# Sliding-window attention and a channel mix on one core: which transposes go through the DMA crossbar

## The chip, the cores and the metric

The kernel runs on one core of one Trainium2 chip. A core has five engines with instruction queues of their own: TensorE (PE, matrix products; its weight loads are listed apart as PEld), VectorE (DVE), ScalarE (ACT), GpSimd (POOL) and SyncE (SP), which here only issues DMAs. Sixteen DMA engines do the transfers. The metric is device microseconds of one execution; lower is better.

## The reference

Attention over four batches and eight heads with 768 positions of 64 values; a position sees itself and the 127 before it, and the first four positions of its batch ("sinks"). Its output, with the heads side by side as 512 columns, is the input x of a channel mix:

```python
scores = scale * np.matmul(q, k.transpose(0, 1, 3, 2))
keep = is_sink | in_window                       # rel >= 0 and rel < 128, or pos < 4
a = softmax(np.where(keep, scores, -1e9))
x = (a @ v)                                      # heads side by side: B x 768 x 512
xk = mu_k * x + (1.0 - mu_k) * x_prev            # x_prev: x of the position before
xr = mu_r * x + (1.0 - mu_r) * x_prev
k = np.maximum(xk @ w_k, 0.0)                    # 512 x 1024
v = k * k @ w_v                                  # 1024 x 512
r = 1.0 / (1.0 + np.exp(-(xr @ w_r)))            # 512 x 512
return r * v
```

## The kernel before

The work is cut into twelve units of 256 positions: unit u is part u % 3 of batch u // 3. For each unit the kernel does the following.

- **Loads.** k, q and v of the unit come in fp32 on SP's queue, two DMAs each (L404 v, L414 and L434 k and q), into `ks`, `qs`, `vs`, which have three buffers each.
- **Casts.** k, q and v are cast to bf16 (`kb`, `qb`, L619 and L626; `vb`, L681), in halves, each on ScalarE, VectorE or GpSimd.
- **Transposes of k and q.** The products need `kt` and `qt` with the 64 values of a head along the partitions. There are two ways. On TensorE: four 128x128 transposes for a half (L654) into a PSUM bank, and a copy out of it (L667) by ScalarE or VectorE; k and q then come in rows of 1 KB (L434). By the DMA crossbar: SP issues one transposing DMA for a half (L641); k and q then come in rows of 256 bytes (L414). `KD` and `QD` say for which units the second way is taken: k of units 4 to 11, q of units 8 to 11.
- **Attention.** Scores (`sc`, L749) two head pairs at a time, exponentials (`e`, L803, ScalarE), a mask (L817, VectorE), products with v (`o` in a bank, L836), a reciprocal (`rec`, L850) and the scaling into `x` (L853), both VectorE. There are four head pairs in a unit.
- **Transposes of x.** `mix` turns x into `xt`, the 512 columns along the partitions: on TensorE, four transposes for a half of x (L877) and a copy out of PSUM (L886, ScalarE or VectorE). The tuple `XD` could name units for the crossbar; it is empty here.
- **Mix.** VectorE forms `td`, the difference of neighbouring positions (L905, two per unit), and from it `xk` and `xr` (L916, four each).
- **Channel mix.** Key products (`kp`, L967), relu (`rl`, L977 ScalarE or L981 VectorE), square (`kk`, L989), gate products (`rp`, L998) with a tanh (`th`, L1004), value products (`vp`, L1016; the last quarter L937), a last combination (`ob`, L1025, L947), and stores on SP's queue (L1032, L952).

The five weight loads stand among the first loads; their casts to bf16 are spread over three engines (L584, L588, L590). Fillers, products of a tile of zeros (L1036), run on TensorE where it would stand in the first part of the kernel.

Every step is first recorded as an operation with a number, in program order. `ORDER` gives, for each engine, the numbers in the order in which that engine is to issue them; `CHOICE` gives the engine of an operation that has a choice; `Plan.schedule` replays the five lines against costs written in the file, only to settle which buffer each tile takes and where fillers go. Engines wait for each other through semaphores alone. So each queue runs strictly in its written order: an instruction that waits holds up all that stands behind it on its engine, and on SP a transposing DMA that waits for its source holds up the loads behind it.

Of the kernel before, what the change touches and what calls it, by code (L numbers as in the profile page):

```python
# [18 lines left out]
    92: "ACT", 93: "ACT", 94: "ACT", 98: "ACT", 102: "DVE", 103: "POOL", 106: "POOL",  # L19
    111: "DVE", 112: "DVE", 113: "ACT", 139: "DVE", 142: "POOL", 151: "ACT", 152:  # L20
    "DVE", 154: "DVE", 198: "DVE", 199: "POOL", 202: "POOL", 206: "ACT", 227: "DVE",
    286: "DVE", 287: "DVE", 288: "ACT", 320: "DVE", 356: "POOL", 358: "POOL", 360:
    "DVE", 366: "ACT", 367: "DVE", 436: "POOL", 438: "DVE", 443: "POOL", 446: "ACT",
    447: "ACT", 449: "DVE", 518: "DVE", 526: "ACT", 527: "ACT", 532: "DVE", 595:
    "POOL", 605: "ACT", 606: "ACT", 608: "DVE", 677: "POOL", 683: "DVE", 684: "ACT",
    686: "DVE", 755: "DVE", 759: "DVE", 761: "ACT", 762: "DVE", 774: "DVE", 830:
    "POOL", 836: "POOL", 838: "ACT", 839: "DVE", 856: "DVE", 916: "DVE", 919: "DVE",
    1014: "DVE", 1038: "DVE", 1042: "DVE",
}

KD = range(4, 12)
QD = range(8, 12)

XD = ()
# [4 lines left out]

BEGIN = {"SP": 800.0, "PE": 1260.0, "ACT": 800.0, "DVE": 930.0, "POOL": 930.0}  # L40

FUDGE = ((42000.0, 900.0), (1e12, 300.0))
# [7 lines left out]
SWITCH = 100.0  # L50

# [5 lines left out]
ORDER = {  # L57
    "PE": (
        104, 101, 88, 117, 107, 110, 115, 128, 120, 125, 143, 153, 131, 140, 136, 149,
        146, 169, 160, 167, 181, 221, 225, 222, 226, 233, 197, 234, 203, 170, 173,  # L60
        178, 182, 185, 190, 207, 249, 194, 214, 229, 230, 200, 251, 314, 306, 315,
        318, 307, 319, 239, 263, 252, 310, 260, 255, 237, 311, 241, 292, 322, 242,
        245, 264, 276, 267, 272, 246, 279, 326, 282, 327, 359, 299, 285, 334, 324,
        330, 364, 331, 345, 410, 382, 337, 390, 383, 386, 391, 342, 387, 412, 353,
        394, 368, 348, 395, 398, 375, 402, 439, 424, 403, 400, 462, 290, 463, 470,
        444, 471, 413, 492, 416, 425, 421, 433, 428, 406, 448, 407, 455, 504, 490,
        466, 474, 519, 467, 475, 480, 478, 529, 545, 549, 546, 550, 486, 524, 557,
        487, 558, 493, 573, 496, 505, 501, 513, 508, 553, 584, 554, 531, 561, 538,
        482, 576, 563, 483, 581, 569, 598, 570, 603, 651, 592, 565, 587, 607, 566,
        649, 663, 621, 633, 625, 614, 622, 626, 634, 639, 637, 629, 652, 630, 660,  # L70
        655, 699, 703, 700, 704, 664, 729, 727, 672, 667, 707, 711, 685, 712, 708,
        692, 641, 730, 741, 733, 738, 642, 645, 715, 766, 646, 780, 792, 781, 788,
        784, 789, 719, 793, 720, 785, 742, 808, 745, 750, 723, 717, 773, 724, 811,
        764, 819, 796, 816, 800, 798, 801, 854, 840, 858, 862, 855, 859, 863, 827,
        884, 882, 804, 866, 822, 805, 872, 867, 870, 847, 885, 896, 888, 893, 878,
        874, 879, 932, 940, 933, 875, 962, 897, 941, 900, 905, 936, 918, 937, 944,
        960, 925, 950, 945, 956, 948, 974, 963, 957, 1000, 966, 1001, 1008, 971, 1009,
        975, 978, 1004, 986, 983, 1005, 1012, 952, 993, 953, 1016, 1018, 1013, 1020,
        1028, 1024, 1032, 1021, 1029, 1025, 1033, 1036, 1040, 1037, 1041, 1048, 1046,
        1044, 1049, 1056, 1052, 1057, 1053,  # L80
    ),
    "DVE": (
        80, 81, 102, 89, 111, 112, 119, 124, 116, 121, 126, 122, 130, 127, 135, 139,
        154, 132, 133, 137, 155, 138, 158, 156, 159, 90, 91, 162, 157, 164, 163, 172,
        165, 166, 177, 189, 227, 198, 152, 184, 174, 179, 175, 180, 186, 191, 187,
        192, 236, 209, 210, 216, 211, 217, 218, 95, 212, 224, 228, 220, 219, 259, 320,
        254, 96, 97, 256, 257, 261, 213, 262, 232, 99, 271, 309, 266, 243, 321, 313,
        317, 268, 273, 269, 274, 247, 294, 287, 295, 297, 328, 360, 301, 286, 303,
        302, 336, 341, 296, 332, 298, 347, 338, 304, 339, 352, 343, 305, 344, 393,
        354, 385, 355, 349, 389, 350, 370, 397, 438, 373, 371, 377, 372, 378, 379,  # L90
        415, 404, 432, 291, 367, 420, 427, 417, 418, 422, 434, 423, 429, 435, 430,
        449, 518, 381, 380, 450, 408, 374, 451, 457, 453, 459, 458, 452, 465, 469,
        530, 473, 477, 500, 460, 512, 507, 495, 454, 488, 552, 497, 498, 502, 514,
        503, 515, 509, 461, 575, 510, 532, 580, 560, 548, 556, 533, 577, 591, 578,
        540, 536, 586, 534, 582, 484, 583, 542, 571, 535, 544, 541, 593, 588, 594,
        608, 543, 567, 589, 659, 654, 609, 537, 610, 616, 612, 618, 619, 611, 666,
        617, 636, 624, 656, 661, 657, 628, 662, 671, 632, 755, 683, 673, 674, 668,
        620, 669, 686, 737, 613, 732, 687, 706, 688, 694, 734, 739, 735, 695, 740,
        643, 696, 689, 690, 702, 647, 759, 698, 710, 768, 744, 714, 691, 771, 697,
        749, 769, 721, 746, 751, 747, 752, 815, 787, 810, 762, 783, 774, 725, 812,  # L100
        765, 775, 813, 770, 791, 795, 777, 817, 776, 818, 802, 772, 779, 821, 826,
        856, 828, 842, 861, 843, 829, 778, 865, 839, 823, 824, 806, 892, 857, 887,
        844, 869, 845, 889, 894, 890, 849, 850, 851, 852, 895, 846, 904, 853, 880,
        899, 876, 916, 935, 901, 906, 902, 907, 919, 970, 943, 920, 939, 927, 923,
        921, 928, 924, 947, 922, 929, 965, 958, 977, 967, 968, 972, 973, 982, 979,
        1011, 980, 1003, 984, 930, 985, 931, 988, 1007, 989, 995, 991, 996, 997, 954,
        990, 992, 1014, 999, 1015, 998, 1022, 1031, 1026, 1035, 1042, 1038, 1039,
        1043, 1050, 1058, 1054,
    ),
    "ACT": (  # L110
        77, 79, 78, 100, 105, 109, 123, 118, 108, 113, 129, 134, 148, 144, 145, 141,
        150, 147, 161, 176, 171, 168, 196, 188, 93, 223, 151, 183, 235, 204, 92, 193,
        208, 250, 215, 195, 231, 94, 258, 201, 253, 308, 316, 206, 240, 270, 265, 312,
        98, 293, 238, 323, 275, 278, 277, 281, 284, 363, 280, 283, 300, 361, 335, 340,
        325, 365, 288, 346, 411, 351, 441, 384, 392, 388, 414, 369, 396, 419, 376,
        399, 440, 431, 426, 401, 366, 464, 445, 472, 499, 516, 494, 446, 521, 456,
        526, 491, 511, 520, 468, 476, 481, 523, 506, 547, 551, 447, 525, 479, 675,
        559, 574, 579, 600, 605, 527, 555, 590, 539, 562, 585, 597, 564, 602, 599,
        604, 653, 658, 679, 650, 665, 606, 615, 681, 623, 635, 627, 640, 638, 753,
        631, 670, 701, 705, 728, 736, 731, 713, 693, 684, 709, 748, 743, 757, 716,  # L120
        761, 834, 767, 782, 790, 794, 814, 786, 809, 718, 832, 825, 797, 799, 838,
        820, 910, 908, 841, 860, 864, 886, 883, 912, 891, 873, 868, 914, 848, 903,
        871, 898, 934, 942, 969, 938, 961, 926, 964, 946, 951, 949, 976, 981, 1002,
        1010, 987, 1006, 994, 1017, 1019, 1030, 1034, 1045, 1047,
    ),
    "POOL": (
        87, 85, 86, 82, 103, 106, 83, 84, 114, 142, 202, 199, 205, 358, 356, 289, 436,
        443, 595, 677, 528, 830, 763, 836, 917,
    ),
    "SP": (  # L130
        1, 0, 2, 3, 4, 5, 8, 9, 6, 7, 10, 19, 20, 11, 12, 13, 17, 18, 14, 21, 22, 15,
        16, 23, 24, 25, 26, 31, 32, 27, 29, 30, 244, 28, 35, 37, 36, 357, 362, 33,
        437, 38, 442, 43, 333, 41, 34, 42, 39, 44, 248, 45, 40, 47, 517, 49, 53, 46,
        329, 522, 48, 51, 405, 596, 50, 676, 489, 601, 55, 54, 52, 56, 485, 61, 57,
        409, 678, 59, 680, 682, 60, 58, 67, 568, 63, 65, 66, 69, 62, 754, 756, 758,
        572, 760, 68, 64, 644, 71, 648, 73, 831, 835, 726, 833, 837, 70, 72, 722, 74,
        909, 803, 75, 807, 911, 913, 915, 76, 881, 877, 955, 1023, 959, 1027, 1051,
        1059, 1055,
    ),
}  # L140


class Plan:

    SEM = 60.0
# [8 lines left out]
    def op(self, engine, cost, emit, rank, reads=(), writes=(), take=(), hold=(), port=False,  # L161
           lag=None, service=0.0, descs=128, mode=0, alts=None, room=2080):
        i = len(self.ops)
# [8 lines left out]
    def schedule(self):  # L172
        ops = self.ops
# [918 lines left out]
```

## Time and profile before

| | |
|---|---|
| runs, us | 170.49, 172.09, 172.26; median 172.09 |
| profiled execution: span, us | 170.4 |
| TensorE busy | 160.5 us (94%), granted clock 0.988 in the mean |
| VectorE busy | 152.1 us (89%) |
| ScalarE busy | 127.3 us (75%) |
| GpSimd busy | 18.9 us (11%) |
| DMA | 33.82 MB, 199 GB/s in the mean |
| transposing DMAs | 16 for k, 8 for q, all on SP's queue |

The profile comes from one execution. A group's busy time counts overlapping instructions once; "mean" is the duration of one. TensorE's instructions are pipelined and their ends are modelled, so a run of matmuls is better priced by the chain of waits, which gives the time from one to the next. A stretch of the table by windows shows busy microseconds of each engine, the granted clock (PEclk) and the mean busy share of the 16 DMA engines, which can pass 1 where packets overlap. "Landing" is the time from the issue of a DMA to its last byte.

### The profile page before, as it was taken

What the parts mean: (1) busy time and instruction counts of PE and PEld (TensorE: products, weight loads), DVE (VectorE), ACT (ScalarE), POOL (GpSimd) and SP (SyncE); (2) the same over time, 40 slices, a digit from 0 to 9 for tenths busy, and PEclk for the clock granted to TensorE, in tenths of its full rate; (3) what the DMA queues carried; (4) which work ended last, traced back from release to release, by engine and by line L of the source; (5) the groups of instructions that cost most, each with busy time, mean ns of one, the idle gap of its engine ahead of it and who ended that gap; (6) DMA issues with size and microseconds to landing.
All of it is one profiled execution on the core that took longest, in us unless ns stands there. A gap on an engine that the chain in (4) does not pass through costs nothing.

```text
span 170.4 us, 4224 instructions
## 1 busy us (share of the span) xinstructions
PE 160.5 (94%) x1598; PEld 103.6 (61%) x1616; DVE 152.1 (89%) x393; ACT 127.3 (75%) x208; POOL 18.9 (11%) x44
## 2 busy tenths in 40 slices
PE   7986998899999999999999999979999999999992
PEld 2444476665658566767557785745575675765751
DVE  5197988999999899999999999898999999999562
ACT  3595799999899999999978989627597648842220
POOL 6720210101430200100020000201000020000000
PEclk9998799999999999999999999999999999999999
DMA  4999989899997999699899896949989750001313
GB/s 137 245 316 348 298 246 257 307 370 304 219 232 167 201 199 276 143 246 189 234 251 208 166 265 140 184 131 296 215 194 231 178 168 8 0 4 62 146 38 123
DMA packets 76803, 33.82 MB, mean 199 GB/s; under 512 B 63848, under 2 KB 71280, under 8 KB 76784
## 3 DMA queue, kind: packets, MB, share of 16 engines
q1 hardware_dynamic: 76768, 33.56, 80.9%
q8 instruction: 12, 0.20, 0.5%
q14 instruction: 7, 0.06, 0.1%
q10 hardware_dynamic: 16, 0.00, 0.0%
HBM read 24.12 MB, written 6.29 MB: 179 GB/s over the span
## 4 chain that ended last, share of the span: by engine, by line
PE 63%; DMA 11%; SPq 9%; DVE 8%; ACT 5%; issue 2%; DVEq 0%
PE bank L1016 18%; PE bank L967 17%; PE bank L998 10%; DMA qs<-in_q_dram 6%; PE sc L749 5%; PE bank L836 5%; DMA ks<-in_k_dram 3%; SPq L414 3%; SPq L404 2%; PE bank L877 2%; DMA qt<-qb 2%; ACT e L803 2%; PE bank L1036 2%; PE bank L654 2%; SPq L434 2%
## 5 line engine op out<-in xcount | busy, mean ns | idle before, releaser
L967 PE MATMUL bank<-xk,wk_sb 128*128 128x256 bf16 x384 | 51.0, 273 | 0.5 <-DVE xk L916 0.4
L803 ACT ACTIVATE e<-sc 128x1024 bf16<-128x1024 f32 (+1 forms) x48 | 44.6, 956 | 4.8 <-PE sc L749 4.7
L1016 PE MATMUL bank<-wv_h,kk 128*128 128x512 bf16 x172 | 45.5, 379 | 0.5
L967 PEld LDWEIGHTS <-wk_sb 128*128 128x128 bf16 x384 | 35.7, 98 | 10.3 <-issue 1.3
L977 ACT ACTIVATE rl<-bank 128x512 bf16<-128x512 f32 x42 | 24.4, 599 | 12.5 <-PE bank L967 10.4
L817 DVE TENSOR_TENSOR e<-e,mask 128x1024 bf16<-128x1024 bf16 (+1 forms) x48 | 30.4, 645 | 0.0
L1016 PEld LDWEIGHTS <-kk 128*128 128x128 bf16 x184 | 16.7, 98 | 13.7
L998 PE MATMUL bank<-wr_sb,xr 128*128 128x512 bf16 x90 | 23.7, 379 | 0.3
L916 DVE SCALAR_TENSOR_TENSOR xk<-td,mu_all,xt 128x256 bf16<-128x256 bf16 x48 | 23.8, 519 | 0.1
L916 DVE SCALAR_TENSOR_TENSOR xr<-td,mu_all,xt 128x256 bf16<-128x256 bf16 x48 | 22.6, 480 | 0.0
L1004 ACT ACTIVATE th<-bank 128x512 f32<-128x512 f32 x24 | 14.2, 604 | 9.0 <-PE bank L998 8.7
L989 DVE TENSOR_TENSOR kk<-rl 128x512 bf16<-128x512 bf16 x48 | 19.1, 415 | 0.7 <-ACT rl L977 0.6
L853 DVE TENSOR_TENSOR x<-bank,rec 128x256 bf16<-128x256 f32 x48 | 19.3, 414 | 0.3
L1025 DVE SCALAR_TENSOR_TENSOR ob<-th,bank 128x512 f32<-128x512 f32 x23 | 15.6, 679 | 3.1 <-ACT th L1004 1.4
L836 PE MATMUL bank<-vb,e 128*128 128x65 bf16 x352 | 16.4, 194 | 0.1
L836 PEld LDWEIGHTS <-e 128*128 128x128 bf16 x352 | 13.8, 97 | 3.3 <-issue 0.5
L749 PE MATMUL sc<-qt,kt 64*128 64x128 bf16 (+1 forms) x256 | 14.2, 242 | 1.2 <-DMA qt<-qb 1.1
L998 PEld LDWEIGHTS <-xr 128*128 128x128 bf16 x96 | 9.0, 98 | 8.9 <-issue 0.3
L749 PEld LDWEIGHTS <-kt 64*128 64x128 bf16 x256 | 9.3, 96 | 6.6 <-issue 4.0
L886 ACT COPY xt<-bank 128x512 bf16<-128x512 bf16 x17 | 10.0, 588 | 3.9 <-PE bank L877 3.8
L1036 PE MATMUL bank<-warm 128*128 128x512 bf16 x35 | 11.8, 485 | 1.1 <-DVE warm L1055 1.1
L905 DVE TENSOR_TENSOR td<-xt 128x512 bf16<-128x512 bf16 x24 | 10.0, 416 | 0.0
(78 smaller groups left out, 153.5 us busy)
## 6 DMA issues: line engine op xcount, KB each, us to landing
qs<-in_q_dram SPq DMA_DIRECT2D x24, 256.0 KB, 4.7
ks<-in_k_dram SPq DMA_DIRECT2D x24, 256.0 KB, 4.3
vs<-in_v_dram SPq DMA_DIRECT2D x24, 256.0 KB, 4.7
out_dram<-ob SPq DMA_DIRECT2D x23, 256.0 KB, 3.7
w<-in_moe_w_k_dram SPq DMA_DIRECT2D x2, 1024.0 KB, 10.5
w<-in_moe_w_v_dram SPq DMA_DIRECT2D x2, 1024.0 KB, 10.2
w<-in_moe_w_r_dram SPq DMA_DIRECT2D x1, 1024.0 KB
kt<-kb SPq DMA_TRANSPOSE x16, 4.0
```

The lines of the kernel that those rows point to most:

```text
L749: nc.tensor.matmul(out=sc[:, a, o0:o1], lhsT=lhs[rows], rhs=rhs[rows], start=u not in BIAS, stop=True, skip_group_check=u in BIAS)
L803: nc.scalar.activation(out=buf[ek][:, :, lo:], in_=buf[sck][:, :, lo:], func=AF.Exp, scale=scale)
L817: nc.vector.tensor_tensor(out=at, in0=at, in1=m, op=ALU.mult)
L836: nc.tensor.matmul(out=o[:, g, a, :], lhsT=e[:, a, e0:e0 + 128], rhs=rhs, start=(T == 0 and i == 0), stop=(i == len(blocks) - 1), skip_gro ...
L853: P.op("DVE", dve(256), lambda ok=ok, rk=rk, c=c: nc.vector.tensor_tensor(out=buf["x", u][:, :, 128 * c:128 * c + 128].rearrange("p g (a d ...
L916: nc.vector.scalar_tensor_tensor(out=buf[key][:, c, :], in0=buf[tk][:, i, :], scalar=mu[w][:, c:c + 1], in1=xt[:, c, t0 - 1:t0 + 255], op0 ...
L967: nc.tensor.matmul(out=ps[:, i, :], lhsT=wk_sb[:, c, 128 * f:128 * f + 128], rhs=xk[:, c, :], start=(c == 0), stop=(c == NC - 1), skip_gro ...
L977: nc.scalar.activation(out=buf[rk], in_=buf[psk].rearrange("p (i t) -> p i t", i=2), func=AF.Relu)
L989: P.op("DVE", dve(512, 0.52), lambda f2=f2, rk=rk: nc.vector.tensor_tensor(out=buf["kk", u][:, 2 * f2:2 * f2 + 2, :], in0=buf[rk], in1=buf ...
L998: nc.tensor.matmul(out=buf[psk], lhsT=buf["xr", u][:, c, 128 * g:128 * g + 128], rhs=wr_sb[:, c, :], start=(c == 0), stop=(c == NC - 1))
L1016: nc.tensor.matmul(out=buf[psk], rhs=wv_h[:, f, :], lhsT=buf["kk", u][:, f, 128 * g:128 * g + 128], start=(f == 0), stop=(f == NF - 1))
L1025: P.op("DVE", dve(512), lambda psk=psk, tk=tk, bk=bk: nc.vector.scalar_tensor_tensor(out=buf[bk], in0=buf[tk], scalar=1.0, in1=buf[psk], o ...
```

## The change

The three sets that choose the crossbar are changed, the tables of choices and orders are replaced, and the replay in `Plan.schedule` goes: one `ORDER` now lists all operations (negative numbers are fillers and their bank), and `SLOTS` gives the buffer of each tile. Cut to its core:

```diff
-KD = range(4, 12)
-QD = range(8, 12)
-
-XD = ()
+KD = range(5, 12)
+QD = (10, 11)
+
+XD = (5, 6, 7, 8, 9, 10, 11)
...
-    def schedule(self):
...
     def run(self):
-        for i in self.schedule():
-            if isinstance(i, tuple):
-                self.fill(i[1])
+        keys = [(name, key) for o in self.ops for name, key in o["take"]]
+        for (name, key), slot in zip(keys, SLOTS, strict=True):
+            self.buf[key] = self.pools[name][slot]
+        for i in ORDER:
+            if i < 0:
+                self.fill(self.pools["bank"][-1 - i])
             else:
                 self.ops[i]["emit"]()
```

For a unit in `XD`, the branch of `mix` that was not taken before is now taken. It issues two transposing DMAs, one for each 128 positions, each reading a whole row of x, so that both wait for all four head pairs:

```python
elif half == 0:
    for g in range(2):
        P.op("SP", 1240.0, lambda g=g: nc.sync.dma_start_transpose(
            out=xt[:, :, t0 + 128 * g:t0 + 128 * g + 128], in_=buf["x", u][:, g, :]),
            ...
            reads=[("x", u, c) for c in range(NP)],
```

Instructions by engine, before and after:

| engine | what | before | after |
|---|---|---|---|
| TensorE | transposes of x (L877) | 96 | 40 |
| | transposes of k and q (L654) | 96 | 120 |
| | fillers (L1036) | 35 | 30 |
| ScalarE | copies of x out of PSUM (L886) | 17 | 8 |
| | casts of k and q for the crossbar (L619) | 16 | 8 |
| | copies of k and q out of PSUM (L662, L667) | 19 | 22 |
| | casts of v (L681) | 14 | 12 |
| | relu (L977) | 42 | 45 |
| VectorE | copies of x out of PSUM (L886) | 7 | 2 |
| | casts of k and q (L619, L623, L626) | 5 | 11 |
| | copies of k and q out of PSUM (L662, L667) | 5 | 8 |
| | relu (L981) | 6 | 3 |
| GpSimd | casts of k, q, v and a weight | 15 | 21 |
| SP | loads in 256-byte rows, k and q (L414) | 24 | 18 |
| | loads in 1 KB rows, k and q from unit 1 (L434) | 20 | 26 |
| | transposing DMAs of k and q (L641) | 24 | 18 |
| | transposing DMAs of x (L897) | 0 | 14 |

One weight cast (`wk`) goes from ScalarE to GpSimd, one (`wv`) from VectorE to ScalarE. Line numbers are those of the kernel before. In the new order of SP's queue the first 16 loads stand as before. Around the x transposes (a pair each, here "x5" for unit 5) the queue reads:

```text
q10 half, x5, store, k8 half, v8 half, k8 half, v7 half,
x6, v9 half, k9 half, kt8 pair, k10 half, v8 half, k10 half, k9 half, v10 half,
x7, store, store, kt9 pair, store, v9 half, k11 half, q10 half, q11 half, kt10 pair,
x8, store, store, q11 half, qt10 pair, v10 half, qt11 half, v11 half, store, kt11 half, k11 half,
x9 (a store between its two), store, kt11 half, qt11 half, v11 half, store,
x10, store, x11, stores
```

All other lines of the three compute engines are reordered too, by a few places in most cases.

## The prediction

> **What bounds the kernel now.** I read the page's busy shares, then busy time by stretches, then the chain of waits, then the groups that the change touches. The sum is made against the profiled execution: a span of 170.4 us, at the low end of the three runs (170.49, 172.09, 172.26); their median lies 1.7 us above it, and I carry that difference over unchanged.
>
> ```profile
> core 0: us, PE busy (x) PEld busy (x) DVE busy (x) ACT busy (x) POOL busy (x), PEclk, DMA share, GB/s
> 20.00:30.00 10.00, 9.25 (x120) 6.92 (x120) 8.99 (x24) 8.96 (x16) 0.61 (x1) 1.00 0.89 237
> 30.00:40.00 10.00, 9.49 (x96) 6.39 (x99) 9.97 (x23) 9.63 (x15) 0.76 (x1) 1.00 0.98 347
> 60.00:70.00 10.00, 9.95 (x127) 7.23 (x127) 9.90 (x27) 9.54 (x16) 0.00 (x0) 1.00 1.03 218
> 110.00:120.00 10.00, 8.79 (x83) 4.97 (x83) 9.20 (x24) 4.71 (x8) 1.38 (x3) 1.00 0.82 207
> 150.00:160.00 10.00, 9.89 (x65) 5.91 (x64) 8.45 (x22) 3.43 (x6) 0.00 (x0) 1.00 0.08 28
> ```
>
> TensorE is full from 40 us on (9.76 to 9.95 of every 10), with one hole at 110 to 120. VectorE is nearly as full until 140, ScalarE only until 80. The DMA engines are full early (share near 1) and idle late (0.08). So TensorE sets the end, with VectorE close behind it.
>
> The hole, in the chain of waits (start, us, what) and in the timeline:
>
> ```profile
> 105.04 4.46 DMA qs<-in_q_dram
> 109.52 0.43 DVE qb L619
> ...
> 111.22 3.15 DMA qt<-qb
> 114.37 0.14 issue
> 114.51 0.51 PE sc L749 x8
> ```
> ```profile
> 114.51 0.51 PE L749 MATMUL sc<-qt,kt 64*128 64x256 bf16 x8 [1.06 <-DMA qt<-qb]
> 115.05 0.81 ACT L803 ACTIVATE e<-sc 128x768 bf16<-128x768 f32 x1 [2.49 <-PE sc L749]
> ```
>
> This is unit 9. The second half of its q was issued at 105.04, behind k and v of unit 10, was cast, and waited for its place in SP's queue until 111.22. TensorE stood for 1.06 us, ScalarE for 2.49.
>
> **The change, part by part.**
>
> ```profile
> L877 PE MATMUL bank<-ident,x 128*128 128x128 bf16 x96 | 9.7, 223 | 0.2
> L654 PE MATMUL bank<-ident,qb 128*128 128x128 bf16 x64 | 6.2, 219 | 0.6 <-POOL qb L626 0.5
> L886 ACT COPY xt<-bank 128x512 bf16<-128x512 bf16 x17 | 10.0, 588 | 3.9 <-PE bank L877 3.8
> ```
> ```profile
> 66.12 0.22 PE bank L877 x4
> ```
>
> *TensorE.* x of seven units: 7 x 8 = 56 transposes go. k of unit 4 and q of units 8 and 9: 24 come. Net 32 fewer. By busy time one is 9.7/96 = 0.10 us, together 3.2; in the dense chain four take 0.22, so 0.055 each, together 1.8. TensorE is dense here, so I take -1.8 and keep 3.2 as the other end.
>
> *The hole.* q of unit 9 now comes in two loads of 1 KB rows that stand in SP's queue ahead of the transposes of k of unit 7, and TensorE transposes it. -1.1, or nothing if another wait takes its place; k of unit 9 (its last issue at 109.29) was earlier than q (111.22), so I take -1.1.
>
> *The start.* The first 16 loads stand in the same order, so the wait for k of unit 1 near 14 us stays. Ten fillers ahead of the second scores of unit 1 become nine; ten took 3.08 us in the chain: -0.3. Early casts change engines (a weight cast to GpSimd, one from VectorE to ScalarE); TensorE loses 1.3 us between 20 and 40, so this is worth between -1.3 and, by symmetry, +1.3. The loads, which are the same, hide it: nothing.
>
> *ScalarE* has 9 evacuations of x, 8 casts of k and q, 2 of v and 2 evacuations after the early transposes fewer, 5 evacuations of k or q and 3 relu more: about 8 us less at some 0.6 us each. It is not full after 80: nothing.
>
> *VectorE.* 5 evacuations of x (0.415), 3 relu (0.684), a weight cast (0.681) and a v cast (0.42) go; 6 casts of k and q (0.42) and 3 evacuations from PSUM (0.69) come: -0.6. But GpSimd has 21 casts instead of 15, and beside a cast VectorE is slower, as the timeline shows:
>
> ```profile
> 44.44 0.85 POOL L619 CAST kb<-ks 128x512 bf16<-128x512 f32 x1 [1.50 <-DMA ks<-in_k_dram]
> ...
> 44.73 0.83 DVE L916 SCALAR_TENSOR_TENSOR xk<-td,mu_all,xt 128x256 bf16<-128x256 bf16 x1
> ```
>
> The median of that operation is 0.477, so 0.35 is lost. Nine of the 15 casts do this, 2.7 us in all or 0.18 for a cast; six more make +1.1. VectorE ends at +0.5, hidden while it is not the bound (four of the twelve stretches of 10 us between 20 and 140 leave it 0.6 us or more); uncovered, +0.5.
>
> *DMA.* Transposes go from 24 to 32, but six of the new ones (x of units 9 to 11) fall after about 129 us, where the share drops. Before that two come net, and six loads change from 256-byte to 1 KB rows. Nothing; bounds are the two issues, +2.5 us of SP's queue, and -2.5.
>
> *The new waits.* SP issues the pair of x transposes when all of x is done:
>
> ```profile
> L641 SPq DMA_TRANSPOSE kt<-kb x16: 1200/1244/3142, 47.7 to 132.0; - x16
> ...
> DMA to landing us min/median/max: 2.4/3.4/5.1
> ```
>
> The second starts 1.25 us after the first, so both land 1.25 + 3.4 = 4.65 us after x (3.65 to 6.35 by the row's ends). VectorE then forms td from them. In the new order its work between the last x and the first td, at the chain's steps (0.33 kk, 0.33 x, 0.40 xr, 0.61 e, 0.09 rec; 0.6 ob and rl), is 5.8, 6.9, 4.2, 4.5, 5.0, 4.1 and 4.1 us for units 5 to 11. The median landing is late by 0.45 (unit 7), 0.15 (8), 0.55 (10) and 0.55 (11): 1.7. Units 10 and 11 fall where DMA is idle and may land at the minimum, which leaves 0.6. TensorE's work from the last value product to the first key product of the unit (0.435 for four key products, 0.865 for four of 512 columns) is 11.4, 12.0, 8.8, 8.8, 11.8, 8.3 and 9.5 us; it needs about 1 us to x, 4.65, and 2.3 for td and xk, together 8.0. So it is just covered. I take +1.0, between 0 and the slower rival's price.
>
> What waits behind x on SP: behind unit 5's pair k and v of unit 8, behind unit 6's k and v of unit 9 and the transposes of k of unit 8, behind unit 7's the transposes of k of unit 9. The last is the tightest: 1 us to x, 2.5 for the pair, 1 for two stores, 2.5 for k's pair, 3.4 to land: 10.4 against TensorE's 11.6 us until the scores of unit 9.
>
> Sum: -1.8 - 1.1 - 0.3 + 1.0 = -2.2; 170.4 becomes 168.2, and the median 172.09 becomes 169.9.
>
> **The rivals.** *VectorE becomes the bound.* For it: 9.90 of 10. Against it: the four stretches with room named above. Then TensorE's 1.8 is worth nothing, the hole's 1.1 is still won and the +0.5 shows: 171.5.
>
> *Slower: the crossbar's landing is too long for its place.* At the row's 5.1 us, units 5 and 7 to 9 come late by 0.55, 2.15, 1.85 and 1.35, 5.9 in all (10 and 11 spared by the idle DMA), and VectorE's queue stands behind each td: -3.2 + 5.9 = +2.7, 174.8. It decides from a landing of about 4.4 us, where units 7 to 9 together cost 3 x (1.25 + 4.4) - 13.7 = 3.2 and eat the gain. For it: the DMA share near 1 in the stretch of units 5 to 7. Against it: the median. [...]
>
> *A larger gain.* If busy time is the right price (3.2), the new waits are nil and the early 1.3 us are won through the lighter ScalarE: -3.2 - 1.1 - 0.3 - 1.3 = -5.9, 166.2.
>
> **Numbers.** Forecast 0.45, larger gain 0.15, VectorE 0.17, slower 0.23. The forecast's own range is 168.0 to 171.3 (waits from 0 to 2.5, another wait for the hole). The range for 8 in 10 is 166.5 to 174.0; it leaves out half of the slower case and the tip of the larger gain. One per cent is what a measurement can tell: 170.4 and 173.8. Faster: 0.15 and four fifths of 0.45, together 0.51. Same: the rest of it and VectorE, 0.26. Slower 0.23.
>
> **What would show it.** In the new profile: 32 fewer transposes and PE's busy time lower by 2 to 3 us; no wait of the scores of unit 9 on a DMA; VectorE waiting for DMA xt ahead of td by about 0.5 us at units 7, 8, 10, 11 and nowhere by 2. The prediction is wrong if td waits over 3 us in sum, if SP stands at an x pair while the next k is missing, or if PE's new holes lie before 40 us, where I priced nothing.

## The result, and the profile after

| | before | after |
|---|---|---|
| median of 4 runs each, us | 171.29 (170.41 to 172.26) | 176.5 (175.64 to 176.92) |
| profiled execution: span, us | 170.4 | 175.2 |
| TensorE / VectorE / ScalarE / GpSimd busy, us | 160.5 / 152.1 / 127.3 / 18.9 | 160.6 / 152.1 / 120.3 / 26.5 |
| DMA hardware queue: share of 16 engines, times span | 80.9%, 137.9 us | 83.1%, 145.6 us |
| last load issued at, us | 134.6 | 139.1 |

The changed kernel is slower: ratio 1.033, 95% interval 1.027 to 1.038. The forecast was 169.9, its range ended at 174.0. Ratios here leave out runs of a slower state and medians do not, so the two can differ by up to a per cent.

The stretches of the changed kernel (columns as in the prediction's first table):

```profile
90.00:100.00 10.00, 9.04 (x89) 6.21 (x89) 8.71 (x24) 7.66 (x13) 0.95 (x1) 1.00 0.81 162
110.00:120.00 10.00, 9.66 (x94) 6.04 (x93) 9.93 (x26) 6.08 (x12) 1.18 (x3) 1.00 0.93 181
120.00:130.00 10.00, 8.46 (x77) 5.03 (x75) 7.42 (x20) 4.76 (x10) 0.00 (x0) 1.00 0.76 176
130.00:140.00 10.00, 8.15 (x73) 4.36 (x68) 7.71 (x21) 6.74 (x10) 0.00 (x0) 1.00 0.95 196
```

The hole at 110 to 120 is filled, and two wider ones are open at 120 to 140, where TensorE and VectorE are idle together: both wait for something else. Who waits for what (us in sum, times, longest), from the table of waits:

```profile
DVE td L769 <- DMA xt<-x: 4.4, 3, 2.5
...
DVE kb L483 <- DMA ks<-in_k_dram: 2.3, 1, 2.3
PE bank L862 <- DVE ob L889: 1.9, 1, 1.9
...
PE bank L831 <- DVE xk L780: 1.5, 3, 0.8
```

Both kinds of wait are for a transfer. VectorE stands at its td for x, and at a cast for k of unit 11; what TensorE needs stands behind VectorE. SP's own timeline shows why they are late:

```profile
112.93 2.08 SPq L278 DMA_DIRECT2D qs<-in_q_dram  x2
115.11 4.36 SPq L505 DMA_TRANSPOSE kt<-kb  x2
119.56 2.52 SPq L761 DMA_TRANSPOSE xt<-x  x2
122.14 1.04 SPq L896 DMA_DIRECT2D out_dram<-ob  x2
123.22 0.46 SPq L278 DMA_DIRECT2D qs<-in_q_dram  x1
123.78 2.65 SPq L505 DMA_TRANSPOSE qt<-qb  x2
126.48 0.58 SPq L268 DMA_DIRECT2D vs<-in_v_dram  x1
127.15 1.22 SPq L505 DMA_TRANSPOSE qt<-qb  x1
128.42 0.57 SPq L268 DMA_DIRECT2D vs<-in_v_dram  x1
129.05 0.57 SPq L896 DMA_DIRECT2D out_dram<-ob  x1
129.73 1.28 SPq L505 DMA_TRANSPOSE kt<-kb  x1
131.06 1.57 SPq L278 DMA_DIRECT2D ks<-in_k_dram  x1
132.73 1.21 SPq L761 DMA_TRANSPOSE xt<-x  x1
```
```profile
123.38 0.43 DVE L769 TENSOR_TENSOR td<-xt 128x512 bf16<-128x512 bf16 x1 [2.48 <-DMA xt<-x]
...
135.77 0.43 DVE L483 CAST kb<-ks 128x512 bf16<-128x512 f32 x1 [2.29 <-DMA ks<-in_k_dram]
...
136.84 1.02 PE L862 MATMUL bank<-wr_sb,xr 128*128 128x512 bf16 x4 [1.85 <-DVE ob L889]
```

x of unit 8 was done at 116.36, but SP was in the middle of two transposes of k that took 4.36 us to issue instead of 2.5, so x went out at 119.56 and 120.83. The second half of k of unit 11 went out at 131.06, behind six transposes issued since 119.56, and landed at 135.7.

The two delays are not of one kind. Of the 4.36 us, the first of the two transposes took 3.05, and the DMA share was 1.23 meanwhile (115.0 to 118.2): the issue was stretched while the engines were full (another long one, 3.22 us at 89.56, saw a share of 0.90). From 119.56 to 131.06 SP issued one DMA right behind the other, the transposes at 1.2 to 1.3 us each, with a share of 0.80: there it was SP's issue time, not full engines, that held the load of k back.

The landing itself is short:

```profile
L761 SPq DMA_TRANSPOSE xt<-x x14: 1191/1262/3224, 82.0 to 155.2; - x14
...
DMA to landing us min/median/max: 2.4/2.7/5.2
```

The first row gives the issue time of one (minimum, median, maximum, in ns): 1.26 us in the median, 3.22 in the longest. The second gives 2.7 us from issue to landing, less than the 3.4 that the prediction took from the rows of k.

### The profile page after: what moved, and what is told of

The parts are those of the page before. It is cut to its first block, busy times and chain, and to the rows that moved or that the text cites. A ratio compares the mean times of both kernels' runs of the same rounds, so it can differ in the third digit from the quotient of the medians.

```text
span 175.2 us, 4174 instructions
## 1 busy us (share of the span) xinstructions
PE 160.6 (92%) x1579; PEld 100.8 (58%) x1579; DVE 152.1 (87%) x392; ACT 120.3 (69%) x195; POOL 26.5 (15%) x50
## 3 DMA queue, kind: packets, MB, share of 16 engines
q1 hardware_dynamic: 76512, 34.61, 83.1%
## 4 chain that ended last, share of the span: by engine, by line
PE 55%; DVE 23%; DMA 11%; SPq 5%; issue 2%; ACT 1%; DVEq 0%; ACTq 0%
PE bank L831 15%; PE bank L880 15%; PE bank L862 8%; DMA ks<-in_k_dram 6%; DMA xt<-x 5%; PE bank L700 4%; DVE xk L780 4%; DVE e L681 4%; PE sc L613 4%; DVE xr L780 3%; DVE ob L889 3%; PE bank L518 3%; DVE td L769 2%; DVE kk L853 2%; PE bank L900 2%
## 5 line engine op out<-in xcount | busy, mean ns | idle before, releaser
L667 ACT ACTIVATE e<-sc 128x1024 bf16<-128x1024 f32 (+1 forms) x48 | 44.3, 955 | 3.6 <-PE sc L613 3.3
L841 ACT ACTIVATE rl<-bank 128x512 bf16<-128x512 f32 x45 | 25.8, 606 | 15.9 <-PE bank L831 14.8
L681 DVE TENSOR_TENSOR e<-e,mask 128x1024 bf16<-128x1024 bf16 (+1 forms) x48 | 30.5, 647 | 0.0
L862 PE MATMUL bank<-wr_sb,xr 128*128 128x512 bf16 x96 | 24.5, 379 | 2.6 <-DVE ob L889 1.9
L780 DVE SCALAR_TENSOR_TENSOR xr<-td,mu_all,xt 128x256 bf16<-128x256 bf16 x48 | 23.3, 502 | 0.0
L780 DVE SCALAR_TENSOR_TENSOR xk<-td,mu_all,xt 128x256 bf16<-128x256 bf16 x48 | 21.8, 487 | 0.1
L853 DVE TENSOR_TENSOR kk<-rl 128x512 bf16<-128x512 bf16 x48 | 20.2, 434 | 1.9 <-ACT rl L841 1.8
L700 PE MATMUL bank<-vb,e 128*128 128x65 bf16 x352 | 16.1, 194 | 0.4 <-DVE ob L889 0.3
L900 PE MATMUL bank<-warm 128*128 128x512 bf16 x30 | 10.6, 489 | 1.1 <-DVE warm L918 1.1
L483 POOL CAST kb<-ks 128x512 bf16<-128x512 f32 x5 | 3.5, 702 | 46.6 <-DMA ks<-in_k_dram 46.6
```

The source lines that it names most:

```text
L667: nc.scalar.activation(out=buf[ek][:, :, lo:], in_=buf[sck][:, :, lo:], func=AF.Exp, scale=scale)
L681: nc.vector.tensor_tensor(out=at, in0=at, in1=m, op=ALU.mult)
L700: nc.tensor.matmul(out=o[:, g, a, :], lhsT=e[:, a, e0:e0 + 128], rhs=rhs, start=(T == 0 and i == 0), stop=(i == len(blocks) - 1), skip_gro ...
L780: nc.vector.scalar_tensor_tensor(out=buf[key][:, c, :], in0=buf[tk][:, i, :], scalar=mu[w][:, c:c + 1], in1=xt[:, c, t0 - 1:t0 + 255], op0 ...
L841: nc.scalar.activation(out=buf[rk], in_=buf[psk].rearrange("p (i t) -> p i t", i=2), func=AF.Relu)
L853: P.op("DVE", dve(512, 0.52), lambda f2=f2, rk=rk: nc.vector.tensor_tensor(out=buf["kk", u][:, 2 * f2:2 * f2 + 2, :], in0=buf[rk], in1=buf ...
```

## The experiments

Three theories stood at the start; the expectations call them Q, X and R. *The queue* (Q): SP issues in order and its transfers have no slack, so what stands behind an x pair, or an x pair behind loads, comes late. *The landing* (X): the crossbar is too slow for the place of x. *The orders* (R): the new orders are worse by themselves. Q2 is the queue again, with SP full as a whole over a long stretch. Later this had to be split into SP's issue time and the work of the DMA engines.

### Mending single holes in the changed kernel

The cast of k of unit 11 that held up VectorE, given to GpSimd:

```diff
-    908: "DVE",
+    908: "POOL",
```

> The changed kernel (176.5 us), with one cast alone moved: the second half of k of unit 11 is cast on GpSimd instead of VectorE. In its trace VectorE stands 2.29 us at 133.5 to 135.8 in front of that cast, because the load came late in SP's queue, and TensorE stands 1.85 us behind VectorE. Theory Q (SP's one in-order queue is the cause: x pairs wait behind loads, loads wait behind transposes, and the engines' in-order queues pass it on): 1.9 us less, 174.6. Theory X (the crossbar's own landing time is too long for the place of td): no change, 176.5 within 0.5. Theory R (the rest of the new orders and casts, GpSimd's above all, costs the time): no change, or slower by up to 0.5 for one more GpSimd cast.

176.06 us (ratio 1.027, 1.020 to 1.035). The hole at 134 is gone, and TensorE has others at 140.6 (1.15 us), at 126.1 (0.45) and, early, where the edit changes nothing, at 33.9 (1.48). By the medians the move was worth 0.4 us, less than these intervals can tell.

In the order of SP alone, the transposes of k of unit 10 behind the pair of x of unit 8:

```diff
-  829, 833, 767, 766,
+  767, 766, 829, 833,
```

> The changed kernel with one move in SP's queue: the pair of x transposes of unit 8 stands ahead of the two transposes of k of unit 10 instead of behind them. In the trace x of unit 8 was done at 116.4, the pair was issued at 119.6 and 120.8 and landed at 123.3; VectorE stood 2.48 us in front of td, TensorE about 2.2 us between 123.6 and 126.5. Theory Q: the pair is issued at 116.4, lands at 120 to 121, and 1.5 to 2.2 us go: 174.3 to 175.0. Theory X: the landing is as long as before and k of unit 10 now lands late, so at most 0.5 less: 176.0. Theory R: no change.

178.23 us (1.041, 1.032 to 1.049). The wait for x shrinks, and the one for k of unit 11 grows. In the waits of this run:

```profile
DVE kb L485 <- DMA ks<-in_k_dram: 3.7, 1, 3.7
...
PE bank L864 <- DVE ob L891: 3.5, 1, 3.5
```

Several such moves at once: loads of v and k of unit 8 behind the x pair of unit 6, k of unit 10 behind that of unit 8, the last half of k of unit 11 earlier, and the x pair of unit 9 without the store between:

```diff
-  57, 54, ... 608, 607,
+  608, 607, 57, 54,
...
-  829, 833, 767, 766,
+  767, 766, 829, 833,
...
-  835, ... 838, 905, 72, 839,
+  835, 72, ... 839, 838, 905,
```

> The changed kernel with SP's queue alone reordered at four places: unit 8's pair ahead of k of unit 10 (as in the run before), two loads of unit 8 (v first half, k second half) behind unit 6's pair, the load of the second half of k of unit 11 some 7 us earlier, and unit 9's pair without a store between and ahead of a transpose of k of unit 11. Theory Q: the waits of td at units 6, 8 and 9 and the one for k of unit 11 go, 4 to 5 us: 171.5 to 172.5. Theory X: about 1.9 for k of unit 11 and nothing else: 174.6. Theory R: 174.6 at best.

176.62 us (1.030, 1.022 to 1.039). In time nothing is won, though VectorE now waits 2.6 us for x at td instead of 4.4, and TensorE's largest hole is 1.0 us instead of 1.9. In the first of these three runs the wait at td is 4.9 us in five places. Moves in SP's order change where the lateness shows; none of the three brought the time back.

### The orders without the crossbar

x of units 5 to 11 back on TensorE inside the new orders, copies by ScalarE:

```diff
-XD = (5, 6, 7, 8, 9, 10, 11)
+XD = ()
```

> The changed kernel with x of all units back on TensorE, evacuated by ScalarE; the rest of the change (k of unit 4, q of units 8 and 9 on TensorE, the new orders and engines) stays. TensorE has 56 transposes more, 3.1 us at 0.055 each. Theory Q: the x waits (4.1 us) and the one for k of unit 11 (1.9, since SP's queue is 14 issues shorter) go: 176.5 - 6.0 + 3.1 = 173.6. Theory X: the x waits go, k of unit 11 does not: 175.5. Theory R: the orders still cost, and the 3.1 us come on top of it: 178 or more.

183.67 us (1.074, 1.065 to 1.082), and it tells nothing of the orders: the new orders leave no PSUM bank free for x, so TensorE stood for the copies, 2.0 us ahead of the key products, 2.0 ahead of the value products and 1.8 ahead of the attention products. Inconclusive.

### Less for SP to issue

The 23 full stores of the changed kernel on GpSimd's queue, and in a second kernel on ScalarE's:

```diff
-                nc.sync.dma_start(out=out[b, s0:s0 + 128, :], in_=buf[bk])
+                nc.gpsimd.dma_start(out=out[b, s0:s0 + 128, :], in_=buf[bk])
```

> The changed kernel with the 23 full stores issued by GpSimd instead of SP; nothing else moves. The last runs showed that moving one x pair ahead in SP's queue makes something else late by as much. Theory Q2 (SP's queue as a whole is full from 64 to 140 us: 20.7 of 24 us of issue time between 116 and 140, against 17.4 before): about 14 stores, some 6 us of SP's time, leave that stretch, the x pairs and the loads and transposes of units 9 to 11 come earlier, 2 to 4 us less: 172.5 to 174.5. Theory R (the new orders cost the time by themselves): 176.5, or a little more for GpSimd's and VectorE's sharing.

> The same with the 23 full stores issued by ScalarE's queue. Q2: the same 2 to 4 us less, minus what ScalarE loses by waiting for the stored tile (it has room after 80 us): 173 to 175. Theory R: 176.5 or more.

176.18 us (1.025, 1.017 to 1.032) and 176.87 (1.025, 1.018 to 1.033): by the ratios 0.7 to 0.8% of the time comes back, and the intervals overlap that of the changed kernel (1.027 to 1.038). A full relief did not follow, but stores on another engine's queue may have costs of their own, and a later run shows that they do on GpSimd (1.022 against 0.9965).

### The same hole in the kernel before

The second half of q of unit 9 loaded right behind the first:

```diff
-  61, ... 62,
+  61, 62,
```

> The kernel before with one load moved in SP's queue: the second half of q of unit 9 directly behind its first half instead of behind the loads of unit 10. If the hole of 1.06 us of TensorE in front of the scores of unit 9 is that load's alone: 1.0 less than before. If another wait takes its place (k of unit 9, whose last transpose is issued at 109.3, or what the earlier load pushes back): no change. This is the gain of 1.1 us that the prediction credited.

170.96 us over ten runs against 171.84: ratio 0.9965, 0.9926 to 1.0005. The wait of 1.1 us is gone from this trace; by the ratio it was worth 0.6 us, and the interval just takes in no change. Of the whole kernels in this study it has the lowest median.

### Transfers that nobody waits for, in the kernel before

Here nothing of the mix or the orders of the engines changes. SP gets 14 transposing DMAs more, where the changed kernel would issue its x pairs; they write a spare tile that nobody reads, and x is still transposed on TensorE.

```diff
+            if u >= 5 and half == 0:
+                for g in range(2):
+                    P.op("SP", 1240.0, lambda g=g: nc.sync.dma_start_transpose(
+                        out=spare[:, :, 128 * g:128 * g + 128], in_=buf["x", u][:, g, :]),
...
```

> The kernel before, with x on TensorE as it is there, and 14 more transposing DMAs on SP's queue that read x of units 5 to 11 when it is done and write a spare tile that nobody reads. So the pairs' load on SP's queue and on the DMA engines is there, and nobody waits for their landing. Q2: SP has some 5 us of room between 116 and 140 and none before; 14 issues of 1.25 us and their waits for x push loads back: 3 to 5 us more, 174.5 to 176.5. Theory X (only the landing ahead of td costs) and R (the orders): 0.5 more at most.

180.84 us (1.051, 1.043 to 1.058). With no reader and in the old orders the transfers alone cost 9 us. Neither the landing of x nor the new orders are needed for such a loss.

Two variants ask what of them costs: pairs that read a piece of w_k, there since the start, so that SP never stands for x; and tiny copies (256 bytes) that would still stand for x and move next to nothing.

```diff
-  in_=buf["x", u][:, g, :]
+  in_=wk_sb[:, 0, 0:512]
```
```diff
-  nc.sync.dma_start_transpose(out=spare[:, :, ...], in_=buf["x", u][:, g, :])
+  nc.sync.dma_start(out=spare[0:1, 0, ...], in_=buf["x", u][0:1, g, 0:128])
```

> The kernel before with the same 14 idle crossbar transposes at the same places of SP's queue as in the run with idle pairs (which cost 8.7 us), but they read a piece of wk that is there since the start, so SP never stands waiting for x in front of them. What they cost SP in issue time (14 x 1.25 = 17 us) and the DMA engines in work stays. If SP's standing at the pairs for x (some 8 us in that run's waits before the last pair) is the price: about 1 to 2 us above before, 173. If the issue time on SP or the work in the DMA engines is the price: 6 to 9 us above, 178 to 181.

> The kernel before with 14 tiny idle copies (256 bytes of x each) at the places of the idle pairs: the waits for x on SP's queue stay, the work of the DMA engines and most of the issue time go. Standing for x is the price: 5 to 9 us above before, 177 to 181. Issue time or DMA work is the price: 0 to 2 us above, 172 to 174. The two runs need not add up to 8.7, if it takes both to empty TensorE's cover.

180.5 us (1.053, 1.046 to 1.060) and 175.52 us (1.026, 1.020 to 1.033). Standing for x is not the price of the pairs: without it the cost is the same. The tiny copies, at 0.58 us of issue each, still cost 4.2 us. In the timelines of the idle pairs and of the tiny copies SP pauses nowhere for more than 0.53 us between 40 us and the last load, so x was there when SP came to it.

Then the transposes on ScalarE's queue, as idle ones in the kernel before and as the real ones in the changed kernel:

```diff
-                    P.op("SP", 1240.0, lambda g=g: nc.sync.dma_start_transpose(
+                    P.op("ACT", 1240.0, lambda g=g: nc.scalar.dma_start_transpose(
```

> The kernel before with the 14 idle crossbar transposes of x issued from ScalarE's queue instead of SP's: the DMA engines do the same work, SP has none of it. If the DMA engines' work is the price: 6 to 9 us above before, 178 to 181. If SP's queue is: 0 to 3 us above, where what is above zero is ScalarE's own issue time (about 1.25 us each, 17 us on an engine that is busy 75% of the time).

> The kernel after, in its own orders, with its 14 transposes of x issued from ScalarE's queue instead of SP's. SP's queue as the cause: loads and k/q transposes no longer stand behind the pairs and the pairs no longer behind loads: 169 to 173. Landing of the crossbar too long, or the new orders themselves, as the cause: 176 to 177, no better. If ScalarE, which must now stand for x and issue 17 us more, becomes the bound: above 177, with TensorE waiting for ScalarE's copies and exponentials.

195.6 us (1.143, 1.136 to 1.151) and 193.16 us (1.126, 1.116 to 1.135). Neither can be read as a test of SP. In the first run SP's transposes of k and q waited for the idle ones to land, which they do not need:

```profile
SPq L510 <- DMA spare<-x: 27.3, 6, 6.5
```

and ScalarE's first pair took 6.3 us from the start of the first issue to the end of the second, 2.5 of them the two issues, after a wait of 3.0 us ahead of it. One of SP's transposes (82.83 to 84.04) went out between the two of that pair, and ScalarE computed nothing for 8.2 us. The run does give the work of one transpose, since they have a queue to themselves:

```profile
q10 hardware_dynamic: 7632, 1.84, 5.8%
```

5.8% of a span of 193.9 us is 11.2 us of all sixteen engines (16 small packets of that queue are in the kernel before too), 0.80 us for each of 14.

### Engines' work or SP's time

Idle plain copies of 256 KB of x, 14 of them at the same places, on SP's queue and on GpSimd's:

```diff
-  P.op("SP", 1240.0, lambda g=g: nc.sync.dma_start_transpose(out=spare[...], in_=buf["x", u][:, g, :])
+  P.op("SP", 600.0, lambda g=g: nc.sync.dma_start(out=spare[:, g], in_=buf["x", u].rearrange("p g c -> p (g c)"))
```

> The kernel before with 14 idle plain copies (256 KB of x into a spare tile, twice a unit for units 5 to 11) on SP's queue at the places of the idle pairs. Work in the DMA engines at least that of the pairs, issue time about 0.6 us each instead of 1.25. Issue time alone as the price (0.5 us for each us of it, by the pairs and the tiny copies): 4 to 5 us above before, the same as the tiny copies. The engines' work as the price: 8 us and more above.

> The same 14 idle copies issued from GpSimd's queue, which is busy 15% of the time or less: the same work for the DMA engines, none for SP. SP's queue as the price: 0 to 1.5 us above before. The engines' work as the price: within 1.5 us of the same copies on SP.

175.73 us (1.032, 1.023 to 1.042) and 176.01 us (1.034, 1.026 to 1.041). The queue makes no difference: with no issue added on SP the same transfers cost the same 5 us (4.8 and 5.1 in the medians). So the DMA engines' work alone is enough to make the kernel slow. A rival is that GpSimd, standing for x ahead of its copies (51.9 us in seven waits), holds up its casts. Its trace leaves little room for that: until 119.9 us the two casts that stand behind copies started only after 4.5 and 3.7 us more of waiting, and TensorE's two largest holes, 1.6 us at 91 and 1.7 us at 116, were open by then, behind a store that took 5.8 us to land and a transpose of q. Only a cast of q at 120.97 followed a pair of copies at once (in the kernel before it stood at 117.01).

```profile
q1 hardware_dynamic: 76768, 33.56, 81.3%
q0 software_dynamic: 1120, 3.67, 6.3%
```

GpSimd's 14 copies are 6.3% of 173.8 us: 0.78 us of all engines each. By packet time, a transposing DMA of 128 KB (0.80 us) was as much work here as a plain copy of 256 KB within SBUF (0.78): for a byte it took the engines twice as long.

The idle pairs once more with the stores on GpSimd's queue, and the version with the lowest median (q of unit 9 moved) with its stores there:

```diff
-                nc.sync.dma_start(out=out[b, s0:s0 + 128, :], in_=buf[bk])
+                nc.gpsimd.dma_start(out=out[b, s0:s0 + 128, :], in_=buf[bk])
```

> The kernel before with the 14 idle transposes on SP, and its 23 full stores on GpSimd's queue instead of SP's: SP gets back some 10 us of issue time for the 17 it lost, the DMA engines' work is as with the idle pairs. SP's issue time as the price: 5 us of the 8.7 come back, 175 to 177. The engines' work as the price: 179 to 181, nothing comes back.

> The best version so far (the kernel before, second half of q of unit 9 loaded right behind the first) with its 23 full stores on GpSimd's queue. TensorE stood still only 6.9 us in sum there from 20 us on, so no theory expects much: SP's issue time as the price gives 169.5 to 171, loads a little earlier; otherwise 171, the same as that version.

180.79 us (1.062, 1.052 to 1.071) and 173.92 us (1.022, 1.015 to 1.029). The first gives nothing back. But the second shows that stores on GpSimd are not free: the same version with stores on SP is at 0.9965. They stand for `ob` there, as the row shows, and a cast of v that started at 136.3 with the stores on SP follows a store at 140.9. Whether that is the whole cost is not shown.

```profile
POOL out_dram L899 <- DVE ob L892: 68.8, 14, 14.9
```

So these two, and the stores on GpSimd above, bound the worth of SP's time only roughly.

### The relief

If the stream of transfers is overfilled, taking work out must bring the time back, in the changed kernel and not in the one before. 14 stores (units 4 to 10) are left out of both; that output stays unwritten, all else is computed. This takes work from the engines, and from SP the issues and its waits for `ob`, so it tests the transfers as a whole.

```diff
-            def store(g=g, bk=bk):
+            def store(g=g, bk=bk, u=u):
+                if 4 <= u <= 10:
+                    return
```

> The kernel after without the 14 full stores of units 4 to 10 (their output is left unwritten, everything else is computed): SP is relieved of some 8 us of issue time and of the waits for ob, the DMA engines of 14 x 256 KB, some 11 us of their work at what the idle copies cost them. The stream without slack as the cause: the last load is issued 4 to 6 us earlier than in the changed kernel (139 us) and the time falls to 170 to 172.5. The new orders or the landing of x as the cause: 175 to 176.5, at most 1 us better.

> The kernel before without the same 14 stores. Its TensorE stands still only 6.6 us in sum after 20 us, and of that one hole (1.1 us at unit 9) comes from a late load. The stream bound before as well: 168 to 170. The stream just fits before, so that relief is worth little: 170.3 to 171.3. The relief of the kernel after should be larger by 3 us and more if the stream is what the change overfilled, and of the same size if it is not.

The changed kernel without them: 171.89 us in the median of ten (168.85 to 173.81), the kernel before beside them 171.47; the ratio, 0.993 (0.986 to 1.000), rests on three of the ten, so no gain over the kernel before is shown. The kernel before without them: 171.63 us, 1.001, 0.997 to 1.005. The same relief is worth 4.6 us to the one and nothing to the other. In the changed kernel's trace the holes at 120 to 140 are closed and the loads are back in time; stretches, the DMA queue and the loads of v (24 of them; ns each, then the first and the last issue in us):

```profile
120.00:130.00 10.00, 9.60 (x85) 5.92 (x84) 8.94 (x25) 6.14 (x11) 0.00 (x0) 1.00 0.83 178
130.00:140.00 10.00, 9.95 (x109) 6.25 (x109) 9.78 (x27) 6.56 (x9) 0.61 (x1) 1.00 0.36 68
```
```profile
q1 hardware_dynamic: 74496, 30.94, 79.9%
```
```profile
L268 SPq DMA_DIRECT2D vs<-in_v_dram x24: 374/596/3494, 3.0 to 134.2; - x24
```

Its x pairs still go over the crossbar, in the new orders, and VectorE now waits 2.0 us at td in sum. With both kernels relieved, their medians lie 0.3 us apart. That closes the landing and the orders, by themselves, as causes of the loss.

### The engines' work side by side

Share of the DMA queues times span, issue time that the additions or removals put on SP (number times the median of their row), the issue of the last load, and the time against before:

| kernel | engines' work, us | on SP, us | last load, us | ratio |
|---|---|---|---|---|
| before | 137.9 | | 134.6 | 1 |
| before, less stores | 128.4 | fewer | 132.3 | 1.001 |
| before, tiny copies | 134.8 | +8 | 139.3 | 1.026 |
| before, copies on SP | 149.0 | +8 | 138.8 | 1.032 |
| before, copies on GpSimd | 152.2 | 0 | 139.8 | 1.034 |
| before, idle pairs | 149.7 | +18 | 146.3 | 1.051 |
| after | 145.6 | +10 | 139.1 | 1.033 |
| after, less stores | 136.1 | fewer | 134.2 | 0.993 |

The table reads like a vessel that is just full. Taking work out of the kernel before wins nothing; with more work, or more on SP (the tiny copies, at 134.8 us of work), the last load and the end move together (the end follows that load by 34 to 37 us in each of these runs). The order of cause is not proved by that alone, as the last load also waits for a buffer that the engines free; the runs that add or remove only transfers settle that the transfers are the cause, not by which of their two prices.

SP's timelines tie the two prices together. The durations of SP's issues ahead of the last load sum to 122.6 us in the kernel before, 134.9 with the idle pairs, 128.1 with the tiny copies, 126.9 with the copies on SP, and 129.2 with the copies on GpSimd, where SP issues nothing more. In these five the last load goes out 10.6 to 12.0 us after that sum. So SP is full in all of them, and in the last of them the work added for the engines alone reached the loads as longer issues on SP. The changed kernel differs: 122.9 us of issues, no more than before, and 16.2 us beside them. Of these, SP stands 3.7 us at 64.2, with a transpose of k whose cast ends on ScalarE at 67.87; the kernel before has no such pause. The relieved kernel has it too (3.5 us at 65.0) and shows no loss, so by itself it costs little; what it costs in the full stream was not tested.

## Why the prediction was wrong

**The step that failed** is the one on DMA: "Nothing; bounds are the two issues, +2.5 us of SP's queue, and -2.5". The runs show that it is the transfers that cost: 14 idle transposes added 9.0 us to the kernel before, and 14 stores left out took 4.6 us from the changed kernel and nothing from the other. The step had two flaws.

It counted transposes by time. Up to 129 us that count came true, 21 before and 23 after. But in SP's order 28 stand ahead of the last load instead of 24, and that load went out 4.5 us later, at 139.1 instead of 134.6.

And it left the engines' work out. Eight transposes more are 8 x 0.80 = 6.4 us of work for all sixteen engines; the trace shows 7.7 (145.6 less 137.9). The prediction had read "full early and idle late" from stretches at 20 to 40, 60 to 70, 110 to 120 and 150 to 160. These rows of the kernel before lay between:

```profile
70.00:80.00 10.00, 9.92 (x111) 6.75 (x110) 9.90 (x26) 9.49 (x18) 0.82 (x1) 1.00 1.14 214
80.00:90.00 10.00, 9.89 (x97) 5.66 (x98) 9.97 (x28) 8.46 (x15) 1.13 (x3) 1.00 1.03 229
90.00:100.00 10.00, 9.95 (x129) 7.65 (x127) 9.85 (x26) 9.05 (x17) 0.00 (x0) 1.00 0.95 194
100.00:110.00 10.00, 9.89 (x99) 6.94 (x99) 9.25 (x26) 8.87 (x14) 0.61 (x1) 1.00 0.88 196
...
120.00:130.00 10.00, 9.90 (x90) 6.45 (x91) 9.95 (x27) 8.12 (x14) 0.00 (x0) 1.00 1.14 204
130.00:140.00 10.00, 9.95 (x115) 6.66 (x115) 9.84 (x26) 5.89 (x10) 0.96 (x1) 1.00 0.67 179
```

The share (the column before GB/s) is at 1.03, 1.14, 1.03 from 60 to 90, at 0.95 to 0.82 from 90 to 120 and again at 1.14 from 120 to 130. The engines were near full until 130, along with TensorE. So was SP: its issues fill 8.8 to 9.6 of every 10 us from 60 to 130. The changed kernel did not get more through: the share times time up to 130 us sums to 127.6 us before and 126.5 after, from 130 to 160 to 8.1 and 16.1. The added work came out at the end, and the loads came late with it.

**The new waits, +1.0.** VectorE waited 4.4 us at td, more than the 3 at which the prediction called itself wrong, but not for its reason. The landing was shorter than assumed (2.7 us against 3.4). "SP issues the pair of x transposes when all of x is done" did not hold: for units 6 and 8 SP was 2.2 and 3.2 us late (87.31 to 89.56; 116.36 to 119.56), since its issues of loads (1.11 us for one of k at 87.40, 0.91 for one of v at 88.55; the median of v's is 0.60) and of k transposes (3.05 at 115.11; median 1.23) stretched. With the stream relieved the waits were 2.0 us, twice the term.

**What waits behind x on SP.** The prediction took k of unit 9 for the tightest; those scores started on time (114.18, before 114.51). The late one was k of unit 11, a load the text did not look at: the sign "SP stands at an x pair while the next k is missing" came true in kind, with a transposing DMA of k ahead of the load.

**TensorE, -1.8 (3.2).** 32 transposes fewer, as said: 192 to 160 in the groups that transpose x, q and k, and their busy time from 19.0 us (9.7 + 6.2 + 3.1) to 16.0 (4.3 + 7.5 + 4.2). TensorE's busy time as a whole did not fall by the 2 to 3 us named as a sign (160.5 and 160.6); the trace before lacks some records (172 of 184 value products), so the totals compare only roughly. What of the term reached the end is not shown: even the relieved kernel, with a median of 171.89 against 171.47, has no clear gain, where the whole sum was -1.3%.

**The start, -0.3 and nothing.** TensorE's busy time in the first 60 us is 55.2 before and 55.0 after, and the first scores of unit 5 start at 63.12 and 63.33. Right within that; the loss comes later: scores of unit 7 at 84.95 (before 86.63), of unit 8 at 101.03 (98.60), of unit 10 at 129.56 (126.26), of unit 11 at 141.42 (137.88).

**The hole, -1.1.** Gone, as said. Its own removal in the kernel before was worth 0.6 us, half the term, in an interval that just takes in no change.

**ScalarE and VectorE.** -8 us and +0.5 were forecast; 7.0 fewer (127.3 to 120.3) and no change (152.1) were measured, and both were hidden. Right.

**The rivals.** The slower one gave 174.8 and so was nearest in time, but its mechanism, a landing of 4.4 us or more, is not what happened. VectorE did not become the bound: it idled with TensorE from 120 to 140. No rival named the work of the DMA engines, and none priced what SP's order does to the loads.

**The range.** The forecast's own range, 168.0 to 171.3, does not follow from the bounds it names: with waits of 0 the sum gives 168.9, with 2.5 it gives 171.4, and with another wait for the hole besides 172.5. The measured time lies above all of these.

**What stays open.** How the loss in the changed kernel divides between SP's time and the engines' work. Either alone makes the kernel before slower (8 us on SP cost 4.2; 11 us of work by GpSimd's own queue row cost 5.1), the two together do not add up (copies on SP cost no more than on GpSimd), and moving the stores off SP brought back no more than 0.8%, with costs of its own. The changed kernel's trace shows both, stretched issues before 119 us and plain issue time after it, and beside them SP's pause at 64.2, whose share of the loss was not tested. Why 14 copies of 256 bytes cost 4.2 us was not tried further.

## What to carry to other kernels

The step that moved here from an engine to DMA had two prices beside its latency (2.7 us): its issue on the queue, 1.26 us of SP for one transpose, and its work on the DMA engines, share times time, 0.80 us of all sixteen, in the very stretch where it lands; both are to be held against every row of the share column, and against what stands ahead of each load in its queue. Transfers that nobody waits for (9.0 us more in the kernel before) and stores left out (4.6 us less in the changed one) told here in two runs that the stream was full, whatever the orders around it. And when mending one hole only opens the next, as in the first three runs here, look upstream, at what feeds them all.

## What the runs showed of the hardware that was not expected

- A transposing DMA of 128 KB took 0.80 us of packet time of all sixteen engines, as much as a plain copy of 256 KB within SBUF (0.78).
- With 14 idle transposing DMAs on ScalarE's queue, SP's transposes of k and q waited for the landing of the idle ones: 27.3 us in six waits, the longest 6.5.
- 14 copies of 256 bytes on SP's queue, 0.58 us of issue each, cost 2.6% (2.0 to 3.3).
- Issuing a pair of transposes took 2.5 us at 119.56 us in the changed kernel, and 4.36 us at 115.11, with a DMA share of 1.23 over the longer issue.
- With 14 plain copies on GpSimd's queue, SP's issues ahead of its last load, the same ones, took 129.2 us in sum instead of 122.6.
